# A decode layer with SyncE's weight stream: 16 small loads added behind it, and 17 one-row loads on GpSimd's queue

## The chip, the core and the metric

The kernel runs on one core of a Trainium2 chip. A core has five engines, each with its own instruction stream: TensorE (PE; its weight loads are listed as PEld), VectorE (DVE), ScalarE (ACT), GpSimd (POOL) and SyncE (SP, which here only starts transfers and waits). They meet through semaphores. Transfers between HBM and the on-chip memory run on 16 DMA engines, fed by queues; each issuing engine has a queue of its own (q1 is SP's, q10 is ACT's; q8 and q14 carry instructions). The metric is the device time of one execution in microseconds. A run's time is a little longer than the profile's span, which goes from the first to the last instruction of the program.

## What is computed

One decode step of a transformer layer for 8 sequences of one token: attention over the last 1024 positions of a cache with 32 query heads and 4 key heads, then a GeGLU feed-forward block. Cut to the core:

```
h = x + A(layernorm(x), k_cache, v_cache, wq, wo)      # x: [8, 1, 1024]
    q = (x @ wq) -> 32 heads of 128
    k, v = the last 1024 of 4096 positions, 4 heads, each repeated 8 times
    o = softmax(q k^T / sqrt(128)) v;   A = o @ wo
out = h + B(layernorm(h), w_gate, w_up, w_down)
    B = (gelu(x @ w_gate) * (x @ w_up)) @ w_down       # 1024 -> 3584 -> 1024
```

All is fp32. The weights and the cache, 111 MB, are read once; the arithmetic on 8 rows is small.

## The kernel before

The kernel is written engine by engine, with its waits by hand. `Flow.run` (lines 81 to 87) starts an instruction on an engine behind given semaphore values and counts the engine's own semaphore up; `Flow.move` (lines 89 to 92) starts a transfer, on SP unless told otherwise, with a semaphore of its own that reaches 16 when all has landed. `Flow.start` (lines 72 to 79) puts the waits ahead of the instruction on the engine that issues it, so whatever comes later on that engine stands behind these waits.

Weights stream through one large on-chip buffer `space` with two halves (lines 116 to 134). In order, each as a transfer from SP: two halves of wq (8 MB each), two of the keys, two of the values, two of wo, then four transfers of the GeGLU weights: gate and up for the first 4 blocks of 512 columns (8 MB each), gate and up for the other 3 blocks (6 MB each). A transfer waits until TensorE has read what stood in its place before.

The GeGLU loop (lines 365 to 407) has two rounds, k = 0 and k = 1; in each, s = 0 is the gate and s = 1 the up projection. `used[k, s]` is the moment when TensorE has done the matmuls of that transfer. So `used[1, 0]` stands for the end of the gate matmuls of the second round, after which ACT applies gelu while the up weights are still on the way.

The down projection's 28 row blocks come in six transfers `wd0` to `wd5` of 8, 8, 4, 4, 2 and 1 blocks (`PARTS`, lines 424 to 443); the last block is loaded in two halves `we0` and `we1` (`ends`, lines 444 to 449). For row block 19 the last 320 columns are left out of their transfer and come instead in eight small transfers of 4 rows by 5 KB into `w_side` (lines 430 to 438). All of these are issued by SP, in the order of the code, each behind the `used` value of the place that it overwrites. So SP issues the last five only when `used[1, 1]` is reached.

TensorE then accumulates the row blocks as they arrive (lines 452 to 500): blocks 0 to 25 into `ya`, block 26 and the sum of `ya` into `acc` and `tb`, and at the end block 27 from `we0` and `we1`. ACT copies the two results into `o_fin`; SP stores the first half (`out0`) and ACT the second (`out1`). SP finally clears all semaphores and waits for the two stores (lines 508 to 516).

GpSimd fills constants at the start (lines 141 to 176) and has nothing to do afterwards.

Of the kernel before, what the change touches and what calls it, by code (L numbers as in the profile page):

```python
# [7 lines left out]
P = 128  # L8
# [23 lines left out]
TAIL = 2  # L32


SLOW = (*range(0, 8), 16, 17)


class Flow:
# [42 lines left out]
    def run(self, engine, make, *waits, mark=True):  # L81
        ins = self.start(engine, make, waits)
        if not mark:
            return None
        self.done[engine] += 1
        ins.then_inc(self.own[engine], 1)
        return self.own[engine], self.done[engine]

    def move(self, name, out, src, *waits, engine="sync"):
        s = self.sem(name)  # L90
        self.start(engine, lambda e: e.dma_start(out, src), waits).then_inc(s, 16)  # L91
        return s, 16


def decode_block(nc, x, wq, kt, v, wo, gu, dn, side, ends, outs):
# [8 lines left out]
    fl = Flow(nc)  # L104
# [5 lines left out]
    def sb(name, *shape):  # L110
        return nc.alloc_sbuf_tensor(name, list(shape), F32).ap()
# [45 lines left out]
    h_sb = sb("h_sb", P, D)  # L157

    w_side = sb("w_side", 64, len(SIDE_ROWS), SIDE_COLS)
    zero = [run("gpsimd", lambda e, t=t: e.memset(t, 0.0)) for t in (*qz, h_sb, w_side)]  # L160

    spread = sb("spread", P, CP, B)
# [89 lines left out]
    for hf in range(2):  # L252
        s_ps = big[hf]
        k_t, k_in, wb = load(kt[hf], f"kt{hf}", "s b k", s=2, b=B)
        for b in range(HB):
            for k0 in range(0, W, N):
                for r in range(NQ):
                    s, half = divmod(r, 2)
# [37 lines left out]
    for hf in range(2):  # L296
# [8 lines left out]
        for c in range(KC):  # L305
            for r in range(NQ):
                s, half = divmod(r, 2)
# [54 lines left out]
    used = {}  # L362
    for k, nb in enumerate(SETS):
        pair = big[1 - k].rearrange("p (s n) -> p s n", s=2)
        clear = (ps[1][1], h_ok)[k]
        for s in range(2):
            if k == 0:
                w, w_in, wb = load(gu[k][s], f"gu{k}_{s}", "c n", c=NC)
            else:
                n = NC * nb * N  # L370
# [20 lines left out]
        if k == 1:  # L391

            g, i = divmod(SIDE - q0, N // P)
# [22 lines left out]
    def slot(q):  # L416
        return (base + q) % SLOTS
# [6 lines left out]
    for i, n in enumerate(PARTS):  # L424


        a, b = slot(q0), slot(q0) + n
        clear = used[0, 1] if a >= base else used[1, 0] if b * D <= place // 2 else used[1, 1]
        assert b <= SLOTS and (a >= base or b <= base)
        if q0 <= SIDE < q0 + n:  # L430
            assert SIDE == q0 + n - 1

            side_in = fl.sem("w_side")
            for h, src in enumerate(side):
                p0 = h % 4 + 32 * (h // 4)
                fl.start("sync", lambda e: e.dma_start(w_side[p0:p0 + 13:4], src), [zero[-1]]).then_inc(
                    side_in, 16)
            side_in = side_in, 16 * len(side)
            here = move(f"wd{i}", space[:, a * D:b * D - SIDE_COLS], dn[i], clear)
        else:  # L440
            here = move(f"wd{i}", ring[:, a:b], dn[i], clear)
        arrived.update((q, here) for q in range(q0, q0 + n))
        q0 += n
    blocks = []
    c0 = 0
    for i, (n, src) in enumerate(zip(ENDS, ends)):
        t = rows_of(last)[:, NQ * c0:NQ * (c0 + n)]
        blocks.append((c0, n, t, move(f"we{i}", t, src)))
        c0 += n


    for ch in range(2):
        run("tensor", lambda e: e.matmul(
# [3 lines left out]
    for q in range(0, first, 2):  # L457
        for i in range(NQ):
            e2, ch = divmod(i, 2)
            r = ch if q in SLOW else i  # L460
            n = N - SIDE_COLS if (q + e2, ch) == (SIDE, 1) else N
# [44 lines left out]


    issued = fl.sem("issued")
    nc.scalar.sem_inc(issued, 1)
    nc.sync.wait_ge(issued, 1)  # L510
    late = [s.num for s, val in sent]
# [91 lines left out]
```

## Time and profile before

| what | value |
|---|---|
| median of 3 runs | 265.39 us (265.34 to 265.43) |
| span of the profiled execution | 263.8 us |
| granted TensorE clock, mean | 0.819 |
| PE busy | 137.9 us (52%) |
| DVE, ACT, POOL busy | 23.3, 10.9, 5.5 us |
| moved | 111.44 MB, mean 422 GB/s |
| SP's queue q1 | 3088 packets, 98.0% of 16 engines' span |

The share of a queue is the time that its packets took, out of the time of 16 DMA engines. A packet is one contiguous piece of a transfer, here mostly a row of a weight tile, or a 4-byte completion that counts a semaphore up. A window of the transfer view lists the packets that start in it, with their whole duration, so that the share of a short window can be above 100%. "PE big L376" is the matmul of line 376 that writes the tile `big`; "x48" is the number of instructions; a name behind "<-" in a row of waits is what released the engine.

### The profile page before, as it was taken

What the parts mean: (1) busy time and instruction counts of PE and PEld (TensorE: products, weight loads), DVE (VectorE), ACT (ScalarE), POOL (GpSimd) and SP (SyncE); (2) the same over time, 40 slices, a digit from 0 to 9 for tenths busy, and PEclk for the clock granted to TensorE, in tenths of its full rate; (3) what the DMA queues carried; (4) which work ended last, traced back from release to release, by engine and by line L of the source; (5) the groups of instructions that cost most, each with busy time, mean ns of one, the idle gap of its engine ahead of it and who ended that gap; (6) DMA issues with size and microseconds to landing.
All of it is one profiled execution on the core that took longest, in us unless ns stands there. A gap on an engine that the chain in (4) does not pass through costs nothing.

```text
span 263.8 us, 2071 instructions
## 1 busy us (share of the span) xinstructions
PE 137.9 (52%) x958; PEld 40.2 (15%) x958; DVE 23.3 (9%) x55; ACT 10.9 (4%) x17; POOL 5.5 (2%) x15
## 2 busy tenths in 40 slices
PE   0015806804905906806707707718509676589875
PEld 0011201201201301301202202112102111123122
DVE  0320100100010020200200100160000200010001
ACT  1110000000010020110000000020000000000000
POOL 8000000000000000000000000000000000000000
PEclk9999975985985895975975956986965979599999
DMA  8998998999799989999998999999899989999995
GB/s 318 482 437 358 477 477 378 420 467 477 328 467 477 420 388 457 470 388 437 447 477 348 460 457 437 398 437 477 360 422 455 477 365 465 412 422 452 390 415 203
DMA packets 3256, 111.44 MB, mean 422 GB/s; under 512 B 392, under 2 KB 648, under 8 KB 1072
## 3 DMA queue, kind: packets, MB, share of 16 engines
q1 hardware_dynamic: 3088, 111.22, 98.0%
q8 instruction: 7, 0.11, 0.2%
q10 hardware_dynamic: 160, 0.10, 0.1%
q14 instruction: 1, 0.01, 0.0%
HBM read 111.18 MB, written 0.13 MB: 422 GB/s over the span
## 4 chain that ended last, share of the span: by engine, by line
DMA 78%; PE 20%; SPq 0%; issue 0%; ACT 0%
DMA w<-gu 20%; DMA w<-wq 16%; DMA w<-kt 12%; DMA w<-wo 11%; DMA w<-v 11%; DMA w<-dn 9%; PE big L376 6%; PE big L261 4%; PE tb L233 4%; PE tb L308 3%; PE ya L336 3%; SPq L91 0%; PE acc L485 0%; ACT o_fin L500 0%; PE tb L485 0%
## 5 line engine op out<-in xcount | busy, mean ns | idle before, releaser
L376 PE MATMUL big<-w,ln_t 128*32 128x512 f32 x224 | 36.1, 730 | 21.6 <-DMA w<-gu 21.6
L261 PE MATMUL big<-w,qz 128*32 128x512 f32 x128 | 18.8, 753 | 20.2 <-DMA w<-kt 20.2
L336 PE MATMUL ya<-w,ot 128*32 128x512 f32 x128 | 18.1, 729 | 19.6 <-DMA w<-wo 19.6
L462 PE MATMUL ya<-w,at 128*32 128x512 f32 (+1 forms) x104 | 16.4, 590 | 3.6 <-DMA w<-dn 3.6
L376 PEld LDWEIGHTS big<-w,ln_t 128*32 128x32 f32 x224 | 9.0, 130 | 47.3 <-issue 25.8
L308 PE MATMUL tb<-w,pt 128*32 128x512 f32 x64 | 9.1, 732 | 9.8 <-DMA w<-v 9.8
L233 PE MATMUL tb<-w,ln_t 128*32 128x512 f32 x64 | 9.2, 743 | 9.2 <-DMA w<-wq 9.2
L308 PE MATMUL acc<-w,pt 128*32 128x512 f32 x64 | 8.5, 694 | 8.6 <-DMA w<-v 8.6
L233 PE MATMUL acc<-w,ln_t 128*32 128x512 f32 x64 | 8.6, 699 | 7.5 <-DMA w<-wq 7.5
L188 PE MATMUL ta<-ident,ln_xn 64*128 64x64 f32 x16 | 2.1, 304 | 19.3 <-DVE ln_xn L214 19.3
L261 PEld LDWEIGHTS big<-w,qz 128*32 128x32 f32 x128 | 4.8, 135 | 33.6 <-issue 23.4
L336 PEld LDWEIGHTS ya<-w,ot 128*32 128x32 f32 x128 | 5.0, 132 | 31.2 <-issue 31.2
L462 PEld LDWEIGHTS ya<-w,at 128*32 128x32 f32 x104 | 4.2, 109 | 15.4 <-issue 10.3
L389 DVE TENSOR_TENSOR hm<-ge,big 128x512 f32<-128x512 f32 (+1 forms) x2 | 1.4, 686 | 56.7 <-PE big L376 56.7
L270 DVE TENSOR_REDUCE nmax<-big 128x1 f32<-128x1024 f32 x2 | 2.5, 1225 | 35.7 <-PE big L261 35.7
L272 ACT ACTIVATE p<-big,nmax 128x1024 f32<-128x1024 f32 x2 | 2.2, 1114 | 78.1 <-DVE nmax L270 78.1
L308 PEld LDWEIGHTS tb<-w,pt 128*32 128x32 f32 x64 | 2.5, 131 | 15.7 <-issue 15.7
L188 PEld LDWEIGHTS ta<-ident,ln_xn 64*128 64x128 f32 x16 | 1.7, 200 | 20.1 <-DVE ln_xn L214 20.1
L233 PEld LDWEIGHTS tb<-w,ln_t 128*32 128x32 f32 x64 | 2.3, 134 | 15.5 <-DMA w<-wq 9.4
L308 PEld LDWEIGHTS acc<-w,pt 128*32 128x32 f32 x64 | 2.4, 126 | 14.1 <-issue 14.1
L233 PEld LDWEIGHTS acc<-w,ln_t 128*32 128x32 f32 x64 | 2.4, 126 | 13.0 <-issue 13.0
L205 ACT ACTIVATE ln_sd<-ln_ve 64x1 f32<-64x1 f32 x2 | 0.4, 203 | 69.3 <-DVE ln_ve L204 69.3
(81 smaller groups left out, 53.3 us busy)
## 6 DMA issues: line engine op xcount, KB each, us to landing
w<-gu SPq DMA_DIRECT2D x2, 6144.0 KB, 23.7
w<-dn SPq DMA_DIRECT2D x2, 4096.0 KB, 27.1
w<-dn SPq DMA_DIRECT2D x1, 2048.0 KB, 20.0
w<-dn SPq DMA_DIRECT2D x1, 1888.0 KB, 24.1
w<-dn SPq DMA_DIRECT2D x1, 1024.0 KB, 22.1
w<-dn SPq DMA_DIRECT2D x1, 512.0 KB, 22.9
w<-ends SPq DMA_DIRECT2D x2, 256.0 KB, 23.1
w_side<-side SPq DMA_DIRECT2D x8, 20.0 KB
```

Of the source, the lines that this page charges most:

```text
L188: tok = run("tensor", lambda e, i=i: e.transpose(t[:, i, :], src[:, i * P:(i + 1) * P], ident[:rows, :rows]), id_ok, ready, clear, mark=(i ...
L205: tok = run("scalar", lambda e: e.activation(sd, ve, AF.Sqrt), tok)
L233: tok = run("tensor", lambda e, c=c, j=j: e.matmul(q_ps[32 * j:32 * j + 32, :], xt[c], w[:, c, j * N:(j + 1) * N], start=(c == 0), stop=(c ...
L261: tok = run("tensor", lambda e: e.matmul(s_ps[32 * r:32 * r + 32, k0:k0 + N], qz[hf][:, s, c0:c0 + 32], k_t[:, s, half * HB + b, k0:k0 + N ...
L270: tok = run("vector", lambda e: e.tensor_reduce(out=nmax, in_=s_ps, axis=AX.X, op=ALU.max, negate=True), tok)
L272: p_ok = run("scalar", lambda e: e.activation(p_sb, s_ps, AF.Exp, bias=nmax, accum_out=tot), tok)
L308: tok = run("tensor", lambda e: e.matmul(o3[32 * r:32 * r + 32], pt[:, c, 32 * r:32 * r + 32], v_t[:, s, c, half * HB:(half + 1) * HB, :], ...
L336: tok = run("tensor", lambda e: e.matmul(ya[32 * r:32 * r + 32, :], ot[:, 2 * hf * REP + h + e2].rearrange("p r b -> p (r b)"), w[:, h + e ...
L376: tok = run("tensor", lambda e: e.matmul(pair[32 * j:32 * j + 32, s, :], ht[c], w[:, c, j * N:(j + 1) * N], start=(c == 0), stop=(c == NC ...
L389: tok = run("vector", lambda e: e.tensor_mul(hm[:rows], ge[:rows], pair[:rows, 1, :]), tok, g_ok)
L462: tok = run("tensor", lambda e: e.matmul(ya[32 * r:32 * r + 32, 0:n], at[:, q + e2, :], rows_of(q + e2)[:, ch * N:ch * N + n], start=(r no ...
```

## The change

A buffer `probe` of 2 KB per partition is added. After the down projection's transfers in the code, GpSimd issues 17 loads of one row into its partitions 0 to 16, of 2 to 18 elements (8 to 72 bytes); the first waits for `used[1, 0]`. After `we1`, SP issues 16 loads of 16, 15, ... 1 rows of 32, 31, ... 17 elements into its partitions from 32 on, without a wait. They all read the small tensor `side`, and what they load is used by nothing. Behind the issue of the stores, SP waits until both groups have landed, before it clears the semaphores. All other instructions stand as before, in the same order on every engine.

```diff
+LANES = 16
...
+def flat_rows(side):
+    return side[0].rearrange("p s n -> (p s) n")
...
     w_side = sb("w_side", 64, len(SIDE_ROWS), SIDE_COLS)
+    probe = sb("probe", P, 16, 32)
...
         arrived.update((q, here) for q in range(q0, q0 + n))
         q0 += n
+    single = fl.sem("single")
+    for i in range(LANES + 1):
+        fl.start("gpsimd", lambda e: e.dma_start(
+            probe[i:i + 1, 0, 0:2 + i], side[0][0:1, 0, 0:2 + i]), [used[1, 0]]).then_inc(single, 16)
...
         blocks.append((c0, n, t, move(f"we{i}", t, src)))
         c0 += n
 
+
+    stair = fl.sem("stair")
+    for i in range(LANES):
+        k = LANES - i
+        nc.sync.dma_start(
+            probe[32:32 + k, i, 0:32 - i], flat_rows(side)[0:k, 0:32 - i]).then_inc(stair, 16)
...
     issued = fl.sem("issued")
+    nc.sync.wait_ge(single, 16 * (LANES + 1))
+    nc.sync.wait_ge(stair, 16 * LANES)
     nc.scalar.sem_inc(issued, 1)
     nc.sync.wait_ge(issued, 1)
```

## The prediction

> **What bounds the kernel now.** I read the chain of waits first, then the table of stages, then short windows of the transfer view, because the change adds only transfers. The chain, in order of time (start, length, what):
>
> ```profile
> 204.63 22.79 DMA w<-gu
> 227.46 8.77 PE big L376 x48
> 237.10 22.92 DMA w<-dn
> 260.06 0.43 PE acc L485 x8
> 261.60 0.48 ACT o_fin L500 x2
> ```
>
> From 204.6 us on the kernel waits for weights, but for one stretch of matmuls, 227.5 to 236.2, during which the transfers run on. The stages (bounds, length, busy times of the engines, clock, share of the 16 DMA engines, GB/s) say so:
>
> ```profile
> 221.00:227.00 6.00, 0.69 (x6) 0.00 (x0) 0.00 (x0) 0.59 (x1) 0.00 (x0) 0.75 1.06 453
> 227.00:236.00 9.00, 8.54 (x48) 2.05 (x48) 0.00 (x0) 0.00 (x0) 0.00 (x0) 0.79 0.95 408
> 236.00:251.00 15.00, 12.45 (x79) 3.49 (x76) 1.24 (x2) 0.26 (x1) 0.00 (x0) 1.00 1.01 431
> 251.00:261.00 10.00, 7.90 (x76) 2.43 (x80) 0.75 (x2) 0.00 (x0) 0.00 (x0) 1.00 0.90 370
> ```
>
> A transfer counts where it starts, hence shares above 1. The engines are full from 221 to 251, and only in the last ten microseconds does the share fall. What falls is this: not all 16 engines (I call them lanes) finish together. Window 260.15 to 260.55, while the last two weight loads (we0, we1) run:
>
> ```profile
> q1 hardware_dynamic: 58, 0.11, 71.3%
> ```
>
> 71.3% of 16 is 11.4, so about 11 lanes still work and 5 are done. Whatever delays one of the 11 moves the end; whatever lands on the 5 alone, up to their lead, does not. And what is put on all lanes between 221 and 261 moves the end by its whole cost.
>
> Where the lead comes from shows in one instruction fetch, on its own queue: window 46.0 to 48.0, then the one packet that starts between 47.15 and 47.25, behind it on the same lane by its start, then the usual packets of that size in the window 9.8 to 10.2, and last rows of 16 KB in the window 252 to 254:
>
> ```profile
> q8 instruction: 1, 0.02, 3.2%
> ...
> q1 hardware_dynamic: 1, 0.07, 185.4%
> ...
> q1 hardware_dynamic: 14, 0.92, 529.1%
> q10 hardware_dynamic: 8, 0.00, 1.1%
> ...
> q1 hardware_dynamic: 55, 0.88, 102.9%
> ```
>
> 3.2% of 16 x 2.0 us is 1.02 us for a 16 KB fetch, where a 16 KB weight row takes 102.9% x 32 us / 54 = 0.61 us (the 55th packet is a completion). The next 64 KB row takes 185.4% x 1.6 us = 2.97 us, and the usual one 529.1% x 6.4 us / 14 = 2.42 us. So this fetch costs its lane 0.41 us too much for itself and 0.55 us for the row behind it, beside its bytes.
>
> **The change, part by part.** *Price of a small packet.* The q10 row above holds the completions of the load of x, 8 of them: 1.1% x 6.4 us / 8 = 9 ns each, while the weight rows around them keep 2.42 us. The data of that load, window 7.2 to 7.6, and the start of out0, window 262.7 to 263:
>
> ```profile
> q10 hardware_dynamic: 8, 0.03, 19.9%
> ...
> q1 hardware_dynamic: 96, 0.05, 53.4%
> ```
>
> 19.9% x 6.4 us / 8 = 159 ns for 4 KB; 53.4% x 4.8 us / 96 = 26.7 ns for 512 B. A packet of a few bytes thus lies between 9 and 26.7 ns, and a second queue of eight such pairs beside the weight stream cost nothing but its own durations.
>
> *How many.* The page's count of packets under 512 B fits one completion for each lane that a load uses (21 of SP's transfers on 16 lanes, eight of 4 rows on 4, x on 8, out1 on 16: 336 + 32 + 8 + 16):
>
> ```profile
> DMA packets 3256, 111.44 MB, mean 422 GB/s; under 512 B 392, under 2 KB 648, under 8 KB 1072
> ```
>
> *GpSimd's 17 loads.* They wait for used[1, 0], the matmuls of the third GeGLU transfer, which end just before ACT reads them at 221.75. As built, a row of n elements is n pieces of 4 bytes for n = 2 to 16, one piece for 17, and 9 pieces of two for 18: 135 + 1 + 9 = 145 data packets. Completions lie between 145 (one per piece) and 17 x 16 = 272. Per lane, if spread evenly, that is 18.1 to 26.1 packets, at 9 to 26.7 ns: 0.16 to 0.70 us, and all of it in the full stretch, so all of it on the path. Most packets are 4 bytes, so I go by the 9 ns row, with a little for the data: **0.3 us**. The Trainium skill, "DMA: Bandwidth & Descriptors", section "Why a DMA increments its semaphore by 16 and not by 1", says that a load issued from GpSimd posts a completion on all 16 engines whatever its shape; by that the count is 272 and the sum 0.23 to 0.70 us, by the rule of the rows above it is 145 and 0.16 to 0.48 us. No row here holds a load issued from GpSimd.
>
> GpSimd itself did its last work at 5.9 us (first row below), so nothing queues behind these loads on it. Issue takes 0.35 to 1.14 us each by the nearest rows:
>
> ```profile
> 5.91 0.32 POOL L175 TENSOR_TENSOR add<-ident 128x64 f32<-128x64 f32 x1
> 1.71 1.14 ACTq L91 DMA_DIRECT2D x_sb<-x  x1
> 221.75 0.59 ACT L386 ACTIVATE ge<-big 96x512 f32<-96x512 f32 x1 [32.96 <-PE big L376]
> 222.11 5.08 SPq L436 DMA_DIRECT2D w_side<-side  x8
> 237.57 0.91 SPq L91 DMA_DIRECT2D w<-ends  x2
> 261.95 0.35 SPq L91 DMA_DIRECT2D out<-o_fin  x1
> ```
>
> 17 times that is 6 to 19 us: issued by 228 to 241. The new wait on "single" comes behind out0's issue, so nothing but the clearing of semaphores and the final waits stands behind it.
>
> *SyncE's 16 loads.* They are issued from 238.5 us (the ends' issue over), each at 0.455 us (ends, 0.91 / 2) to 0.64 us (w_side, 5.08 / 8): 7.3 to 10.2 us, over by 249. Behind them on SP stands only out0, and there SP has been waiting for ACT anyway:
>
> ```profile
> SPq L75 <- ACT o_fin L500: 23.4, 1, 23.4
> SPq L516 <- SPq L516: 1.1, 2, 0.9
> ```
>
> So issue costs nothing, with 12 us of cover; without it, 7 to 10 us. Their packets stand behind we1's in the same queue. They number 136 data and, one per lane used, 136 completions; if the small loads always use the same first lanes, the fullest lane has 16 of each: 16 x 26.7 + 16 x 9 ns = 0.57 us at most. They run after the last weights, and window 261.3 to 262.7 holds no packet of q1 or q10 at all, only this one:
>
> ```profile
> q14 instruction: 1, 0.01, 1.9%
> ```
>
> So they have 1.4 us of empty lanes before out0's packets and cost **0**; without the gap, up to 0.57 us. Two more waits on SP at the end are met by then and pass while SP waits 0.9 us for out0 to land: **0**.
>
> **Sum.** The profiled span is 263.8 us, the median of the runs 265.39, so 1.6 us lie around the span and I leave them as they are. 265.4 + 0.3 + 0 + 0 = 265.7 us. A difference of 0.2% (0.53 us) is what the runs can tell from no change.
>
> **Rivals.**
>
> *B: the tiny reads of GpSimd's queue are not hidden.* If each 4-byte piece holds its lane as the fetch did for itself, 0.41 us, and a lane has 145 / 16 = 9.06 pieces, that is 3.7 us on every lane: 265.7 + 3.7 = 269.4 us, slower. It decides as soon as a piece costs 0.03 us more than its packet (9 x 0.03 = 0.27, and 0.3 + 0.27 passes 0.53). For it: a fetch from another queue did pay this. Against it: x's eight loads, also from another queue in a full stream, did not. Chance 0.20.
>
> *C: each of the 17 loads stops each lane as a fetch does, before and behind.* 17 x (0.41 + 0.55) = 16.3 us: 282 us. For it: the fetch, the only queue here that is neither SP's nor ACT's. Against it: a fetch moves 16 KB, these move some bytes. Chance 0.08.
>
> *E: a further instruction fetch.* 18 more instructions stand on SP and 17 on GpSimd. The profile has these fetches over the whole span:
>
> ```profile
> PE 137.9 (52%) x958; PEld 40.2 (15%) x958; DVE 23.3 (9%) x55; ACT 10.9 (4%) x17; POOL 5.5 (2%) x15
> ...
> q8 instruction: 7, 0.11, 0.2%
> q14 instruction: 1, 0.01, 0.0%
> ```
>
> Seven for TensorE's 1,916 matmuls and weight loads is one in some 270 instructions, so 18 hardly bring another. If one comes, its lane loses 1.02 + 0.55 = 1.6 us, hidden in part on one of the 5 early lanes, whole on one of the 11: 267.3 us. Chance 0.07.
>
> *F: SP is late at the end.* Either GpSimd needs over (263.5 - 221.7) / 17 = 2.46 us a load, so that "single" is not met when out0 has landed (at 3 us each: 17 x 0.54 = 9 us, 275 us), or SP cannot put so many loads behind unfinished ones and stalls before out0 (up to 10 us, 276 us). Against the first: no issue here took over 1.14 us. Against the second: the two ends went out in 0.91 us with the eight w_side loads and six more still open or just issued. The Trainium skill, "DMA: Bandwidth & Descriptors", section "Anatomy of one DMA", gives about 2.0 us of fixed cost for a load from GpSimd, mostly until it has landed; were GpSimd to wait that out each time, the estimate by that page is 34 us, over at 256, still no delay. No run here shows it. Chance 0.05.
>
> *G: no cost or a small gain,* because the packets fall into pauses of the lanes. The stage 251 to 261 with its share of 0.90 speaks for pauses, but the 11 late lanes have none to give. Time 265.4, a gain over 0.53 us only if the order of packets happens to help. Chance 0.05.
>
> **The numbers.** The forecast (packets at their own price) has 0.55; its own range is 265.5 to 266.1. Range: from 265.3 (G's side) up to 269.5, so as to hold B and E; C, F and half of G lie outside, together about 0.16. Faster by over 0.2%: most of G, 0.04. Slower: B, C, F, most of E (0.06) and the quarter of the forecast's own chance whose sum lies above 0.53 us (0.14): 0.53. The rest, 0.43, is no change. The likeliest single case stays 265.7, though the cases beside it are nearly all dearer.
>
> **What would show it.** Right: a new queue with some 290 to 420 packets, 9 to 27 ns each; weight rows beside them at their usual length; the last w<-dn landing 0.2 to 0.7 us later than 260.0; the small SP loads' packets between we1 and out0; SP still waiting over 10 us for o_fin. B shows as packets of the new queue near 0.4 us, C as weight rows lengthened by half a microsecond 17 times, E as a further row of q8 or q14 before 261, F as SP's final wait growing or o_fin's wait gone. The forecast fails if the new queue's share between 222 and 245 exceeds 0.5 us per lane.

## The result and the profile after

The changed kernel takes 266.98 us (median of 5 runs, 266.94 to 268.52) against 265.39 us (5 runs, 265.30 to 265.51): 1.6 us more, ratio 1.0074, 95% interval 1.0052 to 1.0096. The time lies inside the stated range (265.3 to 269.5), but 1.3 us above the forecast of 265.7 us and outside the range that the forecast gave itself (up to 266.1). The profiled execution has a span of 265.6 us, 1.8 more than before.

First the chain of waits after, in the rows that answer to those of before:

```profile
204.58 22.90 DMA w<-gu
227.52 8.66 PE big L384 x48
237.05 24.13 DMA w<-dn
261.23 0.42 PE acc L503 x8
262.80 0.48 ACT o_fin L518 x2
```

Up to 237 us nothing has moved. The wait for the last part of the down projection ends at 261.18 us instead of 260.02, and `o_fin` begins 1.20 us late (262.80 against 261.60). The span is 1.8 us longer, so some 0.6 us come in behind `o_fin`. There are two places to explain: about 1.2 us in the weight stream and 0.6 us at the end.

The new queue, from the page of the kernel after, then GpSimd's and SP's issues, SP's waits, and the landing of `out0` in the kernel after and in the one before:

```profile
q0 software_dynamic: 544, 0.00, 0.1%
...
222.06 8.85 POOL L454 DMA_DIRECT2D probe<-side  x17 [215.83 <-PE big L384]
222.16 5.08 SPq L444 DMA_DIRECT2D w_side<-side  x8
238.47 15.53 SPq L467 DMA_DIRECT2D probe<-side  x16
263.15 0.37 SPq L98 DMA_DIRECT2D out<-o_fin  x1
...
SPq L82 <- ACT o_fin L518: 9.1, 1, 9.1
SPq L530 <- DMA probe<-side: 1.7, 1, 1.7
...
out<-o_fin SPq DMA_DIRECT2D x1, 64.0 KB, 2.3
...
out<-o_fin SPq DMA_DIRECT2D x1, 64.0 KB, 1.6
```

GpSimd's 17 loads made 544 packets, which is 17 x 16 x 2: two on each lane for each load, whatever its length. SP took 15.5 us to issue its loads instead of 7 to 10, but they were out by 254.0 us, and SP still waited 9.1 us for `o_fin`: the cover held. New is the last row of the waits: after `out0`'s issue SP stands 1.7 us for its own small loads, which the prediction had long landed. And `out0` itself takes 2.3 us to land instead of 1.6, which answers to the 0.6 us at the end.

Windows of the transfer view show how the two queues share a lane. In 230 to 234 us, of the kernel after and then of the one before:

```profile
q1 hardware_dynamic: 56, 1.84, 106.5%
q0 software_dynamic: 57, 0.00, 0.8%
...
q1 hardware_dynamic: 57, 1.87, 108.5%
```

One packet of q0 for each weight row: a lane takes the queues in turn. A q0 packet takes 0.8% x 64 us / 57 = 9 ns, and the 32 KB rows are not touched: 106.5% x 64 / 56 = 1.217 us, before 108.5% x 64 / 57 = 1.218. This is the picture of the forecast. The Trainium skill, "DMA: Bandwidth & Descriptors", section "Queues, rings and completion order", says that each engine goes round the queues that have work and takes a whole packet, typically of some 9 to 17 descriptors (each the order for one contiguous piece), from one before it turns to the next. The going round agrees, 56 against 57; the size of a turn differs here, since by these counts a turn of SP's queue is one 32 KB row. The reader should note the consequence. GpSimd had issued everything by 231 us, but 34 packets on a lane need 34 turns, 41 us at 1.2 us a row; the last of them in fact passed at 255.3 us, because the later rows are shorter. So the queue was not empty when the short rows came.

There the picture breaks. Rows of 15,104 bytes (`wd2`) in the window 247.1 to 247.5, of the kernel after and then of the one before:

```profile
q1 hardware_dynamic: 9, 0.14, 97.3%
q0 software_dynamic: 6, 0.00, 0.8%
...
q1 hardware_dynamic: 12, 0.18, 106.1%
```

97.3% x 6.4 us / 9 = 0.69 us a row; before, 106.1% x 6.4 / 12 = 0.566. The q0 packets still take about 9 ns each. What is dear is not their record but some of the weight rows just behind `w_side`'s loads: of the 128 rows of `wd2`, 20 take over 0.62 us (up to 0.97), while most keep their length.

### The profile page after: what moved, and what is told of

Read it like the earlier page. It is cut to its first block, busy times and chain, and to the rows that moved or that the text cites. A ratio compares the mean times of both kernels' runs of the same rounds, so it can differ in the third digit from the quotient of the medians.

```text
span 265.6 us, 2105 instructions
## 1 busy us (share of the span) xinstructions
PE 137.1 (52%) x958; PEld 40.1 (15%) x958; DVE 23.3 (9%) x55; ACT 10.9 (4%) x17; POOL 14.4 (5%) x32
## 4 chain that ended last, share of the span: by engine, by line
DMA 78%; PE 20%; SPq 0%; issue 0%; ACT 0%
DMA w<-gu 20%; DMA w<-wq 15%; DMA w<-kt 12%; DMA w<-wo 11%; DMA w<-v 11%; DMA w<-dn 9%; PE big L384 6%; PE big L269 4%; PE tb L241 3%; PE tb L316 3%; PE ya L344 3%; SPq L98 0%; PE acc L503 0%; ACT o_fin L518 0%; PE tb L503 0%
## 5 line engine op out<-in xcount | busy, mean ns | idle before, releaser
L454 POOL DMA_DIRECT2D probe<-side x17 | 8.8, 529 | 215.8 <-PE big L384 215.8
L241 PEld LDWEIGHTS tb<-w,ln_t 128*32 128x32 f32 x64 | 2.2, 130 | 15.5 <-DMA w<-wq 9.5
```

The source lines that it names most:

```text
L241: tok = run("tensor", lambda e, c=c, j=j: e.matmul(q_ps[32 * j:32 * j + 32, :], xt[c], w[:, c, j * N:(j + 1) * N], start=(c == 0), stop=(c ...
L454: fl.start("gpsimd", lambda e: e.dma_start(probe[i:i + 1, 0, 0:2 + i], side[0][0:1, 0, 0:2 + i]), [used[1, 0]]).then_inc(single, 16)
```

## Experiments

All have the kernel before as their base (265.2 to 265.3 us on those chips). Theory T says: what costs is the completions, each holding its lane for 0.1 to 0.2 us unless a longer row hides it. Its rivals are S (SP's stalled issue disturbs the lanes), R (the tiny reads), T' (a share for each GpSimd load wherever it falls) and W (the place that the pieces are written to). Where no row is shown, a time of a single packet or of a single count of a semaphore is read from the packet and semaphore records of the run's trace.

**One group at a time, e1 and e2.** e1 leaves out the block `stair` and its wait, e2 the block `single` and its wait.

> Only GpSimd's 17 loads; SP's 16 loads are left out. The whole change took 266.98 us, 1.59 more than before. Theory T (a completion holds its lane for 0.1 to 0.2 us unless a longer row hides it): the weight stream is as late as with the whole change, the last weight load lands about 1.2 us later than before (five lanes late by some 0.9, all by 0.3), and the end behind it is as before: 266.4 to 266.7 us. Theory S (SP's small loads, whose issue stalled for 4.2 and then 1.2 us at a time while rows were long, disturb the lanes): without them only the packets' own time is left, 265.6 to 265.8 us. Theory R (the tiny reads of GpSimd's pieces are not hidden): as T, but the rows are long on all lanes and not on the four of w_side alone.

> Only SP's 16 loads; GpSimd's 17 are left out. T: the weight stream ends as before; the completions of up to 16 loads on the first lanes, 0.2 us for a load, are still going out when out0's rows arrive, and the first lanes finish the stores up to 0.6 us late: 265.8 to 266.1 us, and SP's last waits grow. S: the rows of the weights around 246 to 251 us are long, the last weight load lands about 0.9 us late: 266.6 to 266.9 us. If SP's packets cost only their 22 ns a pair: 265.4 us.

Measured: e1 266.25 us (266.0 to 268.8, ratio 1.0049, 1.0030 to 1.0068), e2 266.14 us (1.0032, 1.0021 to 1.0043), beside 265.29 us. By the medians each group alone costs some 0.9 us, so the change is two costs and not one. (e1's ratio says more, because three of its 11 runs took 267.3 to 268.8 us.) T had 266.4 to 266.7 for e1 and 265.8 to 266.1 for e2, so it misses both by a little. For e2 the profile answers directly. Its last `w<-dn` wait, SP's wait and the time to landing of out0; then the last `w<-dn` wait of e6 (below; 17 loads on GpSimd, none on SP):

```profile
237.66 22.43 DMA w<-dn
...
SPq L529 <- DMA probe<-side: 1.8, 1, 1.8
...
out<-o_fin SPq DMA_DIRECT2D x1, 64.0 KB, 2.5
...
237.73 23.17 DMA w<-dn
```

With SP's loads alone the weights end at 260.09 us, as before; with GpSimd's alone at 260.90. So S falls. (e1's own profile is of its slowest run, 268.79 us, so e6 stands in for it.) In e2 the stores take 2.5 us to land where they took 1.6: the 0.85 us of e2 is that.

**More bytes with fewer completions, e4; half of the loads, e11.** e4 moves 20.0 KB in one load, the 16 loads 14.3 KB.

```diff
     stair = fl.sem("stair")
-    for i in range(LANES):
-        k = LANES - i
-        nc.sync.dma_start(
-            probe[32:32 + k, i, 0:32 - i], flat_rows(side)[0:k, 0:32 - i]).then_inc(stair, 16)
+    nc.sync.dma_start(
+        probe[32:32 + LANES, :, 0:20],
+        flat_rows(side)[0:LANES, :].rearrange("p (a n) -> p a n", n=20)).then_inc(stair, 16)
```

That is e4. e11 keeps e2's loads and changes their number (and the value waited for):

```diff
-    for i in range(LANES):
+    for i in range(8):
```

> GpSimd's loads are left out, and SP's 16 loads are one load of 16 rows in 16 pieces of 80 bytes each: 256 data packets instead of 136, with one completion for each lane instead of up to 16. T: one completion for a lane is over long before out0's rows: 265.3 to 265.5 us. If the small data packets themselves hold the lanes: as late as the 16 loads, 265.8 to 266.1 us, or later, with more of them on the late lanes.

> GpSimd's loads are left out, and SP issues only the first 8 of its 16 loads (16 to 9 rows). If each load keeps its lanes for 0.2 us behind we1, one after another, the first lanes are done 1.6 us after we1, about when out0's rows arrive: 265.3 to 265.5 us. If the cost goes with the number of loads however the end lies, half of the 0.85 us: 265.7 us.

Measured: e4 265.36 us (1.0002, 0.9993 to 1.0010), e11 265.36 us (1.0004, 0.9995 to 1.0013; one of its 11 runs took 699 us, for a reason that no run shows). More small pieces behind one completion cost nothing, so it is not the pieces. Half the loads cost nothing rather than half, so what counts is whether they are finished before the stores are. e11's rows:

```profile
SPq L529 <- DMA probe<-side: 0.5, 1, 0.5
...
out<-o_fin SPq DMA_DIRECT2D x1, 64.0 KB, 1.6
```

The size of one completion follows from the whole change. Windows 261.85 to 262.2 and 262.2 to 264.0 of the kernel after:

```profile
q1 hardware_dynamic: 56, 0.00, 10.7%
...
q14 instruction: 1, 0.01, 1.6%
```

The last small packets are recorded by 262.2 us at 10.7% x 5.6 us / 56 = 11 ns each, and then q1 has nothing. Yet SP, which issued out0 by 263.52 us, waits 1.7 us more for them, until about 265.2. The last of these packets starts at 262.11 us and the last count of their semaphore comes at 265.23, so the 16 loads of the fullest lane are finished 3.1 us after their packets' records, 0.2 us a load. The counts themselves agree: near the end they come in groups of four, at 264.30 to 264.41, 264.47 to 264.59, 264.65 to 264.76 and 264.83 to 264.95 us, about 0.18 us from group to group, as if four lanes counted one load each in turn. The record of a completion is the time of its descriptor, not the time until its semaphore counts.

The stores show the same. In e2 every packet of theirs has started by 263.47 us, completions included, and twelve lanes have counted both stores by 263.82, but four lanes count them only at 264.13 to 264.69; the counts of the small loads last until 264.34. In e11 these are over at 263.10 us, before the first count of a store at 263.36. ACT's store, on another queue, lands as late as SP's in e2 (2.5 us both), so it is the lane that is behind and not the queue. The Trainium skill, "DMA: Bandwidth & Descriptors", section "Queues, rings and completion order", calls the semaphore increment a strongly ordered write, which lands only after every earlier write from that engine; the lag agrees with it, though no run shows which write is waited for.

**What in GpSimd's loads costs: e5, e6, e7, e8.** In e1's block, e5 makes one load of 16 rows by 16 pieces of two elements; e6 gives all 17 loads 17 elements, which go as one piece; e7 writes to partitions from 64 on; e8 issues six loads.

```diff
e5
-    for i in range(LANES + 1):
-        fl.start("gpsimd", lambda e: e.dma_start(
-            probe[i:i + 1, 0, 0:2 + i], side[0][0:1, 0, 0:2 + i]), [used[1, 0]]).then_inc(single, 16)
+    fl.start("gpsimd", lambda e: e.dma_start(
+        probe[0:16, :, 0:2], flat_rows(side)[0:16, 0:320].rearrange("p (a n) -> p a n", n=20)[:, :, 0:2]),
+        [used[1, 0]]).then_inc(single, 16)
e6
+            probe[i:i + 1, 0, 0:17], side[0][0:1, 0, 0:17]), [used[1, 0]]).then_inc(single, 16)
e7
+            probe[64 + i:65 + i, 0, 0:2 + i], side[0][0:1, 0, 0:2 + i]), [used[1, 0]]).then_inc(single, 16)
e8
+    for i in range(6):
```

> SP's 16 loads are left out, and GpSimd's 17 loads are one load of 16 rows in 16 pieces of 8 bytes: 256 tiny pieces instead of 145, 16 completions instead of 272. Theory T' (the cost goes with the number of loads: each puts a pair of packets, with a completion, on every lane): nothing measurable is left, 265.3 to 265.5 us. Theory R (the tiny reads cost): as much as the 17 loads or more, 266.2 us or above, since there are more pieces.

> SP's 16 loads are left out; GpSimd's 17 loads all have the one row of 17 elements, which goes as a single piece: 17 pieces instead of 145. T': still 17 pairs of packets on each of 16 lanes, 544 packets: as the 17 loads of different lengths, 266.0 to 266.5 us. R: 17 pieces instead of 145 leave little, 265.4 to 265.6 us.

> SP's 16 loads are left out; GpSimd's 17 loads go to partitions 64 to 80 instead of 0 to 16. If the lanes that fall behind do so because the pieces are written where these lanes write (theory W), other lanes fall behind, and those of w_side are spared: 265.6 to 265.9 us. T' and R: no difference from partitions 0 to 16, 266.0 to 266.5 us.

> SP's 16 loads are left out; only the first 6 of GpSimd's loads are issued. Each lane takes one of their packets per weight row (1.2 us here), 12 rows or some 15 us, so they are over at about 242 us, before the short rows of w_side begin at 245. If the cost comes from completions and short rows meeting there (T), 12 x 9 ns = 0.1 us is left: 265.4 to 265.5 us. If each load costs its share wherever it falls (T'), 6/17 of 0.96 us: 265.6 to 265.7 us.

Measured, beside 265.26 us: e5 265.64 (1.0015, 1.0006 to 1.0024), e6 266.12 (1.0035, 1.0022 to 1.0048), e7 266.39 (1.0044, 1.0030 to 1.0058), e8 265.39 (1.0007, 0.9998 to 1.0015). With 17 pieces instead of 145, e6 costs what e1 does: R falls as the account of these 17 loads, and with it rival B of the prediction. W falls with e7. e8's six loads cost 0.13 us, near the 12 x 9 ns = 0.1 us of their packets and below the third of e1 (0.34 us) that T' wants, though its interval reaches up to 0.40 us and so does not exclude T' by itself. The stretched rows of e6, window 247.1 to 247.5, are those of the whole change (106.0% x 6.4 / 10 = 0.68 us for `wd2`'s rows):

```profile
q1 hardware_dynamic: 10, 0.15, 106.0%
q0 software_dynamic: 10, 0.00, 1.4%
```

e5 is a half miss for T': its one load of 256 pieces costs 0.38 us. Its q0 has 32 packets, 16 of 128 bytes and 16 completions, so on this queue one packet can hold many pieces, here 16. The first row is from its page, the others from window 228.04 to 228.55:

```profile
q0 software_dynamic: 32, 0.00, 0.0%
...
q1 hardware_dynamic: 13, 0.43, 242.9%
q0 software_dynamic: 13, 0.00, 3.9%
```

The 32 KB rows beside these packets take 242.9% x 8.16 us / 13 = 1.525 us instead of 1.217. So a packet of 16 tiny pieces goes with some 0.3 us on its lane: tiny pieces are not free. Still, 256 of them in one load cost less than 145 in 17 loads, and e6 says that the pieces are not what the 17 loads pay for.

**Is it the meeting with w_side: e9 and e10.** Both issue `w_side`'s eight loads ahead of the GeGLU weights (the same lines are taken out of the down projection's loop); e9 has no other change, e10 has GpSimd's 17 loads where the change puts them.

```diff
+    side_in = fl.sem("w_side")
+    for h, src in enumerate(side):
+        p0 = h % 4 + 32 * (h // 4)
+        fl.start("sync", lambda e: e.dma_start(w_side[p0:p0 + 13:4], src), [zero[-1]]).then_inc(
+            side_in, 16)
+    side_in = side_in, 16 * len(side)
     at = sb("at", P, DF // P, 32)
```

> Neither group of added loads; the kernel before, with w_side's eight loads issued ahead of the first GeGLU transfer instead of between the down projection's. It is the base for the next run. Both theories: the same bytes on the same lanes, 265.1 to 265.6 us.

> As the run before (w_side's loads early), with GpSimd's 17 loads where the change puts them; SP's 16 are left out. T (GpSimd's packets cost much where they meet w_side's short rows, each with a completion, on four lanes): without that meeting the packets' own 0.3 us is left over the base, 265.5 to 265.8 us, and no lane stalls around 246 us. T' (each load costs its share, wherever it falls): 0.9 us over the base, 266.1 to 266.3 us.

Measured, beside 265.23 us: e9 265.34 (1.0004, 0.9995 to 1.0013), e10 265.75 (1.0017, 1.0008 to 1.0026). Over their own base the same 17 loads now cost 0.41 us instead of 0.96 (no run of e10 is over 266.01 us, none of e1, e6 and e7 under 266.00), and in the window 247.1 to 247.5 the rows of `wd2` have their old length, 89.0% x 6.4 / 10 = 0.570 us, though q0 still sends a packet between each two of them:

```profile
q1 hardware_dynamic: 10, 0.15, 89.0%
q0 software_dynamic: 10, 0.00, 1.4%
```

So over half of the cost is made where q0's packets meet `w_side`'s short rows (before, eight rows of 5 KB, each with a completion of its own, on four lanes). The lanes say so too, by the times at which they count the last `w<-dn` load. Before, the eleven late lanes count it between 259.62 and 260.01 us. In the kernel after, seven do at 259.86 to 260.26 and four at 260.71 to 261.18; in e6, four lie apart in the same way, at 260.61 to 260.91. In e10 none does: eleven lie between 259.86 and 260.55.

How the meeting makes the cost is not shown. The kernel before had w_side's completions spaced by rows of 0.2 us, and the change puts q0's between them. But in the kernel after, the last of GpSimd's loads (its pieces of 8 bytes) passes at 246.46 to 246.89 us on four lanes already, and from 253.15 us on where its other five pieces go, and the longest rows (0.91 to 0.97 us) start at 247.2 to 247.6 us, behind it. So they are not stretched by a q0 packet between them, but after many completions in a short time.

**The same loads early: e3 and e12.** In e1's block only the wait is another, and the block stands earlier in the code.

```diff
e3
-            probe[i:i + 1, 0, 0:2 + i], side[0][0:1, 0, 0:2 + i]), [used[1, 0]]).then_inc(single, 16)
+            probe[i:i + 1, 0, 0:2 + i], side[0][0:1, 0, 0:2 + i]), [q_ok[1]]).then_inc(single, 16)
e12
+            probe[i:i + 1, 0, 0:2 + i], side[0][0:1, 0, 0:2 + i]), [ps[1][1]]).then_inc(single, 16)
```

> Only GpSimd's 17 loads, and they wait for the second half of q (about 53 us) instead of the second round's gate matmuls, so that they pass while all rows are 64 KB and are over before w_side's loads. T: every completion is hidden behind a row of 2.4 us, only the packets' own time is left, 34 x 9 ns = 0.3 us on each lane: 265.6 to 265.8 us. R: a tiny read costs as much there as later: 266.4 us or more. S says nothing of this one beyond its 265.6 to 265.8.

> SP's 16 loads are left out, and GpSimd's 17 wait for the second softmax (about 95 us), between the first early place (53 us) and the change's (222 us); the rows beside them are 64 KB all the way. The early place took 266.14 us, 0.85 more than before, where theory T had 0.3. If that was the price of these loads beside long rows: again 266.0 to 266.3 us, with stretched rows on some lanes between 95 and 180 us. If that was something of that place alone: 265.5 to 265.8 us.

Measured: e3 266.14 us beside 265.29 (1.0037, 1.0023 to 1.0052), e12 266.21 beside 265.23 (1.0036, 1.0023 to 1.0048). T has 0.3 us here and is wrong as it stands: beside rows of 64 KB, away from any short row, the loads cost 0.85 and 0.98 us. T' would fit these two, but not e10's 0.41 us, so neither holds for all runs. e12's windows 150.8 to 152, while q0 runs, and 88.5 to 91, ahead of it:

```profile
q1 hardware_dynamic: 11, 0.72, 150.0%
q0 software_dynamic: 10, 0.00, 0.5%
...
q1 hardware_dynamic: 15, 0.98, 90.8%
```

A 64 KB row takes 150.0% x 19.2 / 11 = 2.62 us there, against 90.8% x 40 / 15 = 2.42. Not every row is stretched: while q0 runs in e12, 45 of 480 rows take over 2.48 us, and the median is 2.42. Why these rows of 64 KB suffer, where those of 32 KB beside the same loads kept their 1.217 us (above), stays open: the early places differ from the change's in the time, the rows and the work beside them, and no run separates these. Rows of 32 KB are not immune either: they took 1.525 us in e5, and up to 1.37 us in the profile of e1's slowest run.

## Why the prediction was right and wrong

Right: the bound. The weight stream and its late lanes set the end, GpSimd's packets lie in the full stretch and are on the path, a packet takes 9 ns, issue on both engines is hidden (GpSimd 8.85 us for 17, SP under its wait for `o_fin`), and more chance stood on slower than on any other outcome. F did not come: GpSimd's issue took 0.52 us a load. Nor did C: the 32 KB rows kept their length, and of the shorter ones a few were stretched, those of `wd2` by up to 0.4 us. E did not come either: the page of the profile lists seven fetches on q8 as before. That the range held the time was luck: it reached to 269.5 us only for B and E, and no rival named what came.

Wrong, first: "They run after the last weights ... and cost **0**" of SP's 16 loads. The step that failed is the price of their packets, 16 x 26.7 + 16 x 9 ns = 0.57 us at most against a gap of 1.4 us. The packets did keep to it, but a load is finished only 0.2 us after the one before on its lane, 3.1 us for 16. That outlasts the gap, and the stores are counted late behind it: 0.85 us alone (e2), nothing when there is one completion (e4) or when the sequence is half as long (e11).

Wrong, second: the term of GpSimd's loads, "**0.3 us**". The count was too low (544 packets, where 290 to 417 were counted), though by the 9 ns row that is still 34 x 9 ns = 0.31 us a lane. What failed is the row it was priced by: the load of x (one load of eight rows, and not eight loads as rival B has it), with one completion on each of eight lanes beside long rows. It does not speak for many completions on a lane, nor for packets that meet short rows. Measured were 0.96 us alone (e1) and 0.41 us with `w_side` out of the way (e10), so 0.55 us are shown to hang on that meeting. The 0.41 us that are left lie within the noise of the forecast 0.3 (the intervals of e9 and e10 are 0.24 us to either side), but e3 and e12 paid 0.85 and 0.98 us without any short row, so 0.3 us is not the price of these loads wherever they fall; why, stays open.

The two sum to 1.8 us, the whole change to 1.6; the intervals of e1 and e2 are wider than the difference.

Also off, without an effect: SP's issue. The first of the 16 loads alone took over 4 us, as the tile's row shows (durations in ns, min/median/max):

```profile
L467 SPq DMA_DIRECT2D probe<-side x16: 296/542/4249, 238.5 to 252.8; - x16
```

The second half of rival F was thus real, and only 9 us of cover kept it off the path.

## What to carry to other kernels

Count a small transfer by its completions and not by its bytes or its packet records: here 0.2 us on each lane for each of SP's loads, one after another, where nothing longer runs between them. One load of more pieces in place of 16 loads cost nothing. Before adding transfers on another queue, look at how long its backlog lasts (one packet a turn, so as many weight rows as packets) and which short rows it will meet on the way. Long rows alone are no cover: beside rows of 64 KB the same 17 loads cost as much.

## What the runs showed beyond that

- A one-row load from GpSimd put two packets on all 16 lanes, even where it was a single piece (e6: 17 pieces, also 544 packets).
- SP stalled 4.2 us in the issue of a small load with the five last weight transfers just issued ahead of it; e4's only load took 4.33 us (its row below), so it is not the number of small loads.

```profile
238.27 4.33 SPq L461 DMA_DIRECT2D probe<-side  x1
```
